# Block attention and feed-forward on one core: loads merged over the two heads of a pair, DMA transposes merged over two pairs, and the value-row transfers issued by SyncE

## The chip, the cores and the metric

The kernel runs on one core of a Trainium2 chip. The metric is the device time of one execution in microseconds (us), lower is better. Three executions of the kernel before took 244.21, 245.65 and 247.01 us, median 245.65. A further execution was recorded by the profiler: 244.68 us in all, of which its trace covers a span of 242.9 us. All times below are counted from the start of that span.

## The reference

Attention over 4 batches of 8 heads, 768 tokens and 64 channels, with a narrow local window (distance below 16) and 24 block summaries beside it; then a feed-forward block over the 3072 tokens with 512 channels in, 2048 hidden and 512 out.

```
k_sum = k.reshape(B, H, nb, 32, D).max(axis=3)          # 24 blocks of 32 keys
v_sum = v.reshape(B, H, nb, 32, D).mean(axis=3)
scores_l = scale * q @ k^T, kept where |i - j| < 16
scores_s = scale * q @ k_sum^T + log(32)
a = softmax(concat(scores_l, scores_s))
x = a @ concat(v, v_sum)
h = x @ w_in;  out = (h * sigmoid(1.702 * h)) @ w_out   # f32 in, f32 out
```

## The kernel before, in words

The work is cut into 8 half batches, u = 0 to 7 (loop at line 896): batch b = u // 2, half = u % 2, each with 384 tokens of all 8 heads. The heads are handled as 4 pairs, p = 0 to 3, since two heads of 64 channels fill 128 partitions.

For each half batch TensorE does first the **in-projection** (ff_in, line 651: tiles ph, 16 hidden tiles of 4 matmuls over the 4 pairs' rows xT) and then the **out-projection** (ff_out, line 679: tiles po, 12 pieces numbered i = 1 to 12 in the loop, four for each of 3 row blocks ms). The attention of the *next* half batch is laid between the pieces of the out-projection, by a table written by hand:

```
plan = {0: ["s0", "s1"], 3: ["v0", "s2", "s3"], 4: ["d0"], 5: ["v1", "d1"]}
```

Here s is the scores of a pair (scores, line 599: TensorE, then the exponential on ScalarE, then the mask on VectorE), v the values of two pairs (values, line 609: TensorE, then the division on VectorE into the tile x), and d the transpose of x by a DMA on SyncE's queue (dx, line 646) into xT, which the next in-projection reads. The first half batches turn x on TensorE instead ("x" in their own tables).

From the third batch on, the inputs of batch b + 1 are made ready while batch b is worked on:

- **Loads** on SyncE's queue: load_k in the out-projection of the second half of batch b - 1 after its first piece, load_v after its eighth piece, load_q only in the first half of batch b, between the transposes of the keys. Each tensor of a batch is 8 loads of 192 KB, one for each head (lines 82 to 114).
- **Casts** to bf16 on GpSimd: keys into kb, values straight into the row table vw, queries into qb.
- **Transposes** by DMA on SyncE's queue: xk (line 566) makes two for each pair, one for each half of the partitions, into kx; xq (line 573) makes one for each pair into qT, at the start of the second half. rest_k (line 577) then puts block maxima and neighbour columns into kx on VectorE.
- **Value rows**: vrows (line 336) sums the value blocks on TensorE (vsum) and VectorE (block_sums, into vs), and copies neighbour rows (vw from vw, 4 transfers) and summary rows (vw from vs, 2 transfers) by DMAs on GpSimd's queue.

Every engine works in the order of the program. SyncE does nothing but issue DMAs, in order: one that is not ready, or that takes long to issue, holds up all that stand behind it. The framework also lets each of SyncE's DMAs wait for the one issued eight places before it. All operations go through one wrapper, so the profile gives nearly all of them line L27; they are told apart by tiles.

Of the kernel before, what the change touches and what calls it, by code (L numbers as in the profile page):

```python
# [10 lines left out]
BF16 = mybir.dt.bfloat16  # L11
# [23 lines left out]
def kernel(  # L35
# [10 lines left out]
    B, H, S, D = q.shape  # L46
# [5 lines left out]
    NP = H // 2  # L52
# [17 lines left out]
    keep = ctx.enter_context(tc.tile_pool(name="keep", bufs=1))  # L70
    stage = ctx.enter_context(tc.tile_pool(name="stage", bufs=1))
    castp = ctx.enter_context(tc.tile_pool(name="cast", bufs=4))
    attp = ctx.enter_context(tc.tile_pool(name="att", bufs=4))
    outp = ctx.enter_context(tc.tile_pool(name="outp", bufs=3))
    psb = ctx.enter_context(tc.tile_pool(name="psb", bufs=2, space=bass.MemoryType.PSUM))
# [3 lines left out]

    raw = {}  # L80

    def load_k(b, p):
        t = stage.tile([128, 2, 2, JH, D], F32, name=f"kf{p}", tag=f"kf{p}")
        for i in range(2):
            if b == 0:
                sp.dma_start(out=t[:, i].rearrange("p h r d -> p h (r d)"),
                             in_=k[b, 2 * p:2 * p + 2, i * HALF:(i + 1) * HALF]
                             .rearrange("h (p r) d -> p h (r d)", r=JH))
            else:
                sp.dma_start(out=t[:, i].rearrange("p e r d -> p (e r) d"),  # L90
                             in_=k[b, 2 * p + i].rearrange("(j p) d -> p j d", p=128))
        raw["k", p] = t

    def load_q(b, p, half=None):
        if half is None:
            t = stage.tile([128, 2, NJ, D], F32, name=f"qf{p}", tag=f"qf{p}0")
            for hh in range(2):
                sp.dma_start(out=t[:, hh],
                             in_=q[b, 2 * p + hh].rearrange("(j p) d -> p j d", p=128))
            raw["q", p] = t  # L100
            return
        t = stage.tile([128, 2, JH, D], F32, name=f"qf{p}{half}", tag=f"qf{p}{half}")
        sp.dma_start(out=t.rearrange("p h r d -> p h (r d)"),
                     in_=q[b, 2 * p:2 * p + 2, half * HALF:(half + 1) * HALF]
                     .rearrange("h (p r) d -> p h (r d)", r=JH))
        raw["q", p, half] = t

    def load_v(b):
        for p in range(NP):
            t = stage.tile([128, 2, NJ, D], F32, name=f"vf{p}", tag=f"vf{p}")  # L110
            for hh in range(2):
                sp.dma_start(out=t[:, hh],
                             in_=v[b, 2 * p + hh].rearrange("(j p) d -> p j d", p=128))
            raw["v", p] = t


# [53 lines left out]
    def finish_masks():  # L170
        masks()

        for t in (0, 4, 6, 8, 10):
# [2 lines left out]
        sel(mk[32:64, NQ - 1, :], 15, 0, -1)  # L176


    kx = [[keep.tile([128, NQ, 128], BF16, name=f"kx{p}_{s}") for s in range(2)]
          for p in range(NP)]  # L180
    qT = [[keep.tile([128, S], BF16, name=f"qT{p}_{s}") for s in range(2)]
          for p in range(NP)]
    vw = [keep.tile([128, NQ, H, VC], BF16, name=f"vw{s}") for s in range(2)]
    vs = keep.tile([128, H, VC], BF16, name="vs")
    vs4 = keep.tile([128, H, VC], BF16, name="vs4")
# [48 lines left out]
                       in_=wo[:, c * 4:(c + 1) * 4, :])  # L234


    cast = {}

    def copy(eng, out, in_):
        if eng is act:  # L240
# [7 lines left out]
    def cast_k(eng, p, half=None):  # L248
        if ("k", p) in cast:
            t = cast["k", p]  # L250
        else:
            t = castp.tile([128, 2, JH, 2, D], BF16, name="kb", tag="kb")
        if half is None:
            copy(eng, t.rearrange("p e r h d -> p h (e r) d"),
                 raw["k", p].rearrange("p h e r d -> p h (e r) d"))
        else:
            copy(eng, t[:, half].rearrange("p r h d -> p h r d"), raw["k", p][:, half])
        cast["k", p] = t
# [4 lines left out]
            cast["q", p, half] = cast.pop(("q", p))  # L263

    def cast_q(eng, p, half=None):
        n = NJ if half is None else JH
        t = castp.tile([128, n, 2, D], BF16, name="qb", tag=f"qb{n}")
        copy(eng, t.rearrange("p r h d -> p h r d"),
             raw[("q", p) if half is None else ("q", p, half)])
        cast["q", p] = t  # L270
# [47 lines left out]
    def halo_dmas(w5, j0):  # L318
        halo_odd(w5, j0)
        halo_even(w5, j0)  # L320
# [15 lines left out]
    def vrows(s):  # L336
        w5 = vw[s].rearrange("p (j e) h c -> p j e h c", e=2)
        halo_odd(w5, 0, pool)
        vsum(s, range(NJ))
        block_sums()  # L340
        halo_even(w5, 0, pool)
        sum_dmas(w5, 0, pool)

    def vrows0():

# [217 lines left out]
        key_rows(p, s, ks)  # L563


    def xk(p, s):
        k4 = kx[p][s].rearrange("p (j e) c -> p j e c", e=2)
        src = cast.pop(("k", p)).rearrange("p e r h d -> p (e r h d)")
        for e in range(2):
            sp.dma_start(out=k4[:, :, e, e * 64:e * 64 + 64],  # L570
                         in_=src[e * 64:e * 64 + 64], transpose=True)

    def xq(p, s):
        sp.dma_start(out=qT[p][s].rearrange("p (j c) -> p j c", c=128),
                     in_=cast.pop(("q", p)).rearrange("p r h d -> p (r h d)"), transpose=True)

    def rest_k(p, s):
        ks = attp.tile([128, nb], BF16, name="ks", tag="ks")
# [317 lines left out]
    for u in range(2 * B):  # L896
        b, half = u // 2, u % 2
        todo = {}
        if u == 0:
            for p in range(NP):  # L900
                cast_q(dve, p, 1)
                todo[4 + p] = [lambda p=p: (q_turn(p, 1), q_copy(p, dve, 1))]
        elif u == 1:
            s = 1
            todo = {2: [lambda: tk(0, s)], 4: [lambda: tk(1, s)],
                    6: [lambda: tk(2, s)], 8: [lambda: tk(3, s)],
                    14: [lambda: halo_odd(w51, 0), lambda: vsum(s, range(NJ))],
                    15: [lambda: block_sums(), lambda: halo_even(w51, 0),
                         lambda: sum_dmas(w51, 0)]}
            for p in range(NP):  # L910
                cast_k(pool, p)
            for p in range(NP):
                cast_v(pool, s, p, 0)
                cast_v(pool, s, p, 1)
            for p in range(NP):
                cast_q1(p)
        elif half == 0 and b + 1 < B:
            s = (b + 1) % 2
            for p in range(NP):
                cast_k(pool, p)  # L920
                xk(p, s)
                if p == 1:
                    for pp in range(NP):
                        load_q(b + 1, pp)
            for p in range(NP):
                cast_v(pool, s, p, 0)
                cast_v(pool, s, p, 1)
            for p in range(NP):
                cast_q(pool, p)
        elif b + 1 < B:  # L930
            s = (b + 1) % 2
            todo = {1: [lambda: xq(0, s), lambda: xq(1, s), lambda: rest_k(0, s)],
                    2: [lambda: xq(2, s), lambda: xq(3, s), lambda: rest_k(1, s)],
                    6: [lambda: rest_k(2, s)], 8: [lambda: rest_k(3, s)]}
# [12 lines left out]
        if nxt:  # L947
            exp_soon()
        i = 0
        order = [(ms, part) for ms in range(JH) for part in range(4)]  # L950
        if u == 0:

            order = [(ms, part) for part in range(4) for ms in range(JH)]
        for ms, part in order:
            if nxt or ms < JH - 1:
                ff_out(u, ms, part)
            elif part == 0:
                ff_last(u, ms)
            if nxt:
                beside(u + 1, i)  # L960
            i += 1
            if u == 0 and i == 1:

                sp.dma_start(out=hold, in_=w_out_sb[0:16, NT - 5, 0:16])
                for p in range(NP):
                    load_k(1, p)
                load_v(1)
                for p in range(NP):
                    load_q(1, p, 0)
                    load_q(1, p, 1)  # L970
            elif half and b + 2 < B and i == 1:
                for p in range(NP):
                    load_k(b + 2, p)
            elif half and b + 2 < B and i == 8:
                load_v(b + 2)
            elif half == 0 and 0 < b < B - 1 and i == 10:
                vrows((b + 1) % 2)


# [28 lines left out]
```

## Time and profile before

| | |
|---|---|
| Median of three runs | 245.65 us (244.21 to 247.01) |
| Profiled execution | 244.68 us, span 242.9 us |
| TensorE busy | 212.7 us, 88% of the span |
| ScalarE, VectorE, GpSimd busy | 137.2, 91.2, 73.7 us |
| Chain that ended last, shares of the span | PE 70%, DMA 12%, DVE 6%, ACT 4%, SyncE's queue 4% |
| of this, the transposes into xT | 7% |
| Moved by DMA | 37.36 MB, 31.50 MB of it on the hardware queue |

The page cuts the span into 40 slices. TensorE's busy digit is 9 in nearly all of them after the first sixth, and falls to 0 and 5 in the neighbouring slices around 106 us and 5 and 0 around 167 us. The chain that ended last follows the work back from the last instruction, at each step to what released it. "SPq" is the issuing of a DMA by SyncE, and the time of a row there runs from the start of its first issue to the end of its last, waits between them included.

### The profile page before, as it was taken

Reading aid. Unit: us, or ns where it says so; the run is one execution under the profiler, and the core shown is the slowest. Engines: PE = TensorE matmul, PEld = TensorE weight load, DVE = VectorE, ACT = ScalarE, POOL = GpSimd, SP = SyncE. Lnnn points to the kernel's source line nnn. Section 1 sums busy time; section 2 is a strip of 40 time slices with the busy share of each in tenths; the row PEclk is TensorE's granted clock in tenths of the full one; section 3 lists DMA queues with packets and bytes.
Section 4 is the critical chain, followed back from the end, with each engine's and each line's share of the span. In section 5 each row is a group of like instructions: output and inputs, shape, how many; then the busy total and the mean of one; then the engine's idle time right before and its main releaser. Section 6 shows DMA issues by size and latency. Waiting matters only on the chain.

```text
span 242.9 us, 5099 instructions
## 1 busy us (share of the span) xinstructions
PE 212.7 (88%) x1989; PEld 119.0 (49%) x1989; DVE 91.2 (38%) x262; ACT 137.2 (56%) x241; POOL 73.7 (30%) x176
## 2 busy tenths in 40 slices
PE   6588899999999999905999999950999999999994
PEld 2556564556554654302555465520465455546543
DVE  5898931559756007470007001673003500530000
ACT  2697466656766788100787278610378557837610
POOL 4569970259434542710230063280000000000000
PEclk9999999999999999975899999995699999999999
DMA  6999999999999979799942795969900510141012
GB/s 172 302 230 234 206 221 178 234 206 263 286 213 219 225 155 209 123 132 238 221 71 78 182 214 110 200 101 183 208 14 0 122 75 0 46 109 45 0 43 86
DMA packets 94487, 37.36 MB, mean 154 GB/s; under 512 B 79664, under 2 KB 91184, under 8 KB 94464
## 3 DMA queue, kind: packets, MB, share of 16 engines
q1 hardware_dynamic: 89600, 31.50, 62.7%
q0 software_dynamic: 4864, 5.55, 14.0%
q8 instruction: 15, 0.25, 0.4%
q14 instruction: 8, 0.07, 0.1%
HBM read 27.26 MB, written 6.29 MB: 138 GB/s over the span
## 4 chain that ended last, share of the span: by engine, by line
PE 70%; DMA 12%; DVE 6%; ACT 4%; SPq 4%; issue 2%; POOL 0%; DVEq 0%; POOLq 0%; ACTq 0%
PE ph L27 31%; PE po L27 31%; DMA xT<-x 7%; SPq L27 4%; PE ps_av L27 3%; PE ps_s L27 2%; DMA vf<-in_v_dram 2%; DMA kf<-in_k_dram 2%; DVE kx L27 1%; DMA qf<-in_q_dram 1%; DVE a_sb L27 1%; ACT a_sb L27 1%; PE ps_k L27 1%; ACT kx L27 1%; PE ps_q L27 1%
## 5 line engine op out<-in xcount | busy, mean ns | idle before, releaser
L27 PE MATMUL ph<-xT,w_in_sb 128*128 128x384 bf16 x512 | 90.8, 337 | 19.1 <-DMA xT<-x 18.6
L27 ACT ACTIVATE gT<-ph 128x384 bf16<-128x384 f32 x128 | 61.9, 490 | 50.0 <-PE ph L27 49.3
L27 PE MATMUL po<-w_out_sb,gT 128*128 128x512 bf16 (+2 forms) x400 | 89.0, 371 | 0.0
L27 PEld LDWEIGHTS <-w_in_sb 128*128 128x128 bf16 x512 | 50.8, 101 | 55.1 <-issue 24.8
L27 PEld LDWEIGHTS <-gT 128*128 128x128 bf16 x400 | 36.4, 98 | 38.5
L27 DVE TENSOR_TENSOR a_sb<-a_sb,mk 128x768 bf16<-128x768 bf16 x32 | 18.6, 585 | 95.4 <-ACT a_sb L27 94.0
L27 ACT ACTIVATE osb<-po 128x512 f32<-128x512 f32 (+1 forms) x24 | 14.2, 592 | 37.1 <-PE po L27 37.1
L27 POOL CAST vw<-vf 128x768 bf16<-128x768 f32 (+3 forms) x35 | 24.8, 736 | 25.3 <-DMA vf<-in_v_dram 24.8
L27 ACT ACTIVATE a_sb<-ps_s 128x768 bf16<-128x768 f32 x32 | 24.3, 806 | 6.7 <-PE ps_s L27 6.7
L27 POOL CAST kb<-kf 128x768 bf16<-128x768 f32 (+1 forms) x13 | 10.6, 817 | 39.2 <-DMA kf<-in_k_dram 29.9
L27 ACT ACT_TABLE_LOAD x16 | 20.5, 1283 | 1.1 <-PEq L992 0.8
L27 POOL CAST qb<-qf 128x384 bf16<-128x384 f32 (+1 forms) x18 | 11.5, 651 | 20.6 <-DMA qf<-in_q_dram 17.4
L27 DVE TENSOR_TENSOR x<-ps_av,rc 128x384 bf16<-128x384 f32 x28 | 15.6, 558 | 1.0
L27 DVE TENSOR_REDUCE ks<-kx 128x24 bf16<-128x768 bf16 x12 | 11.3, 942 | 2.2 <-DMA kx<-kb 2.1
L27 PEld LDWEIGHTS <-a_sb 128*64 128x64 bf16 x384 | 7.9, 111 | 6.9 <-issue 3.8
L27 PE MATMUL ps_av<-vw,a_sb 128*64 128x65 bf16 x384 | 9.9, 198 | 0.4 <-DVE a_sb L27 0.4
L27 DVE COPY osb<-po 128x128 f32<-128x128 f32 x1 | 0.3, 291 | 24.9 <-PE po L27 24.9
L27 DVE COPY kx<-kx 128x80 bf16<-128x80 bf16 (+4 forms) x52 | 9.3, 230 | 0.9 <-ACT kx L27 0.9
L27 PE MATMUL ps_s<-qT,kx 64*128 64x64 bf16 x384 | 9.2, 191 | 0.5 <-ACT qT L27 0.2
L27 PEld LDWEIGHTS <-kx 64*128 64x128 bf16 x384 | 7.0, 95 | 4.8 <-issue 4.0
L27 PEld LDWEIGHTS <-warm 128*128 128x128 bf16 x71 | 5.3, 106 | 7.2 <-issue 5.6
L27 DVE RECIPROCAL rc<-ps_av 128x6 f32<-128x6 f32 x32 | 6.1, 189 | 7.2 <-PE ps_av L27 7.2
(72 smaller groups left out, 123.8 us busy)
## 6 DMA issues: line engine op xcount, KB each, us to landing
kf<-in_k_dram SPq DMA_DIRECT2D x32, 192.0 KB, 3.8
qf<-in_q_dram SPq DMA_DIRECT2D x32, 192.0 KB, 3.9
vf<-in_v_dram SPq DMA_DIRECT2D x32, 192.0 KB, 4.7
out_dram<-osb SPq DMA_DIRECT2D x23, 256.0 KB, 4.4
w_in_sb<-in_moe_w_in_dram POOLq DMA_DIRECT2D x4, 512.0 KB, 7.7
w_out_sb<-in_moe_w_out_dram POOLq DMA_DIRECT2D x4, 512.0 KB, 15.6
vw<-vs POOLq DMA_DIRECT2D x4, 148.5 KB, 7.2
vw<-vw POOLq DMA_DIRECT2D x4, 99.0 KB, 4.1
```

The lines of the kernel that those rows point to most:

```text
L27: r = f(*a, **kw)
```

## The change

- load_k and load_v (for batches 1 to 3) and load_q (for batches 2 and 3) make one load for both heads of a pair: 4 loads of 384 KB for each tensor.
- kx and qT become one tile for all four pairs for each parity of the batch, and the casts of two pairs go into one tile (kb2, qb2), so that xk and xq make one transfer for two pairs: 4 instead of 8 for the keys, 2 instead of 4 for the queries.
- load_q moves ahead: it follows load_v directly, in the half batch before.
- xq moves ahead: from the start of the second half to the tenth piece of the out-projection of the first half.
- The six value-row transfers of batches 2 and 3 are issued by SyncE, behind xq, instead of GpSimd.
- rest_k of the second pair stands one place later (after hidden tile 3 instead of 2).

The core of the diff:

```diff
     def load_k(b, p):
         t = stage.tile([128, 2, 2, JH, D], F32, name=f"kf{p}", tag=f"kf{p}")
-        for i in range(2):
-            if b == 0:
+        if b:
+            sp.dma_start(out=t.rearrange("p h e r d -> p (h e r) d"), in_=chunks(k, b, p))
+        else:
...
     def load_q(b, p, half=None):
         if half is None:
             t = stage.tile([128, 2, NJ, D], F32, name=f"qf{p}", tag=f"qf{p}0")
-            for hh in range(2):
-                sp.dma_start(out=t[:, hh],
-                             in_=q[b, 2 * p + hh].rearrange("(j p) d -> p j d", p=128))
+            sp.dma_start(out=t.rearrange("p h j d -> p (h j) d"), in_=chunks(q, b, p))
...
-    def xk(p, s):
-        k4 = kx[p][s].rearrange("p (j e) c -> p j e c", e=2)
-        src = cast.pop(("k", p)).rearrange("p e r h d -> p (e r h d)")
+
+    def xk(g, s):
+        k4 = kxs[s].rearrange("p i (j e) c -> p (i j) e c", e=2)
+        src = kb2[g].rearrange("p i e r h d -> p (i e r h d)")
         for e in range(2):
-            sp.dma_start(out=k4[:, :, e, e * 64:e * 64 + 64],
+            sp.dma_start(out=k4[:, 2 * g * NJ:2 * (g + 1) * NJ, e, e * 64:e * 64 + 64],
                          in_=src[e * 64:e * 64 + 64], transpose=True)
...
             for p in range(NP):
                 cast_k(pool, p)
-                xk(p, s)
-                if p == 1:
-                    for pp in range(NP):
-                        load_q(b + 1, pp)
+                if p % 2:
+                    xk(p // 2, s)
...
-            todo = {1: [lambda: xq(0, s), lambda: xq(1, s), lambda: rest_k(0, s)],
-                    2: [lambda: xq(2, s), lambda: xq(3, s), lambda: rest_k(1, s)],
+            todo = {1: [lambda: rest_k(0, s)], 3: [lambda: rest_k(1, s)],
                     6: [lambda: rest_k(2, s)], 8: [lambda: rest_k(3, s)]}
...
             elif half and b + 2 < B and i == 8:
                 load_v(b + 2)
+                for p in range(NP):
+                    load_q(b + 2, p)
             elif half == 0 and 0 < b < B - 1 and i == 10:
-                vrows((b + 1) % 2)
+                s = (b + 1) % 2
+                vsum(s, range(NJ))
+                block_sums()
+                xq(0, s)
+                xq(1, s)
+                w5 = vw[s].rearrange("p (j e) h c -> p j e h c", e=2)
+                halo_dmas(w5, 0)
+                sum_dmas(w5, 0)
```

SyncE has 166 rows in its order before and 134 with the change. Two places of that order carry the prediction.

The first is SyncE's queue in the half batch u = 2, ahead of the two transposes into xT that the in-projection of u = 3 reads (kf, vf, qf are loaded inputs, kb and qb their casts, osb a store's source; the numbers at the ends of names are buffers). Before, from the loads of the third pair's queries on:

```order
L27 DMA qf_1555<-in_q_dram 128x6x64 [waits DMAHW4_49]
L27 DMA qf_1555<-in_q_dram 128x6x64 [waits DMAHW5_49]
L27 DMA qf_1558<-in_q_dram 128x6x64 [waits DMAHW6_49]
L27 DMA qf_1558<-in_q_dram 128x6x64 [waits DMAHW7_49]
L27 DMA_TRANSPOSE kx_0_98<-kb 128x6x64 [waits DMAHW0_49,Pool_49]
L27 DMA_TRANSPOSE kx_0_98<-kb 128x6x64 [waits DMAHW1_49]
L27 DMA_TRANSPOSE kx_0_100<-kb 128x6x64 [waits DMAHW2_49,Pool_49]
L27 DMA_TRANSPOSE kx_0_100<-kb 128x6x64 [waits DMAHW3_49]
L27 DMA out_dram<-osb 128x512 [waits DMAHW4_49,Activation_49]
L27 DMA_TRANSPOSE xT_119<-x_1760 128x6x128 [waits DMAHW5_49,DVE_49,PE_49]
L27 DMA_TRANSPOSE xT_120<-x_1836 128x6x128 [waits DMAHW6_49,DVE_49,PE_49]
```

and with the change, from the second pair's queries on:

```order
L27 DMA qf_1453<-in_q_dram 128x12x64 [waits DMAHW4_49,Pool_49]
L27 DMA qf_1455<-in_q_dram 128x12x64 [waits DMAHW5_49,Pool_49]
L27 DMA qf_1457<-in_q_dram 128x12x64 [waits DMAHW6_49,Pool_49]
L27 DMA out_dram<-osb 128x512 [waits DMAHW7_49,Activation_49]
L27 DMA_TRANSPOSE kx_97<-kb 128x12x64 [waits DMAHW0_49,Pool_49]
L27 DMA_TRANSPOSE kx_97<-kb 128x12x64 [waits DMAHW1_49]
L27 DMA_TRANSPOSE kx_97<-kb 128x12x64 [waits DMAHW2_49,Pool_49]
L27 DMA_TRANSPOSE kx_97<-kb 128x12x64 [waits DMAHW3_49]
L27 DMA out_dram<-osb 128x512 [waits DMAHW4_49,Activation_49]
L27 DMA_TRANSPOSE xT_110<-x_1719 128x6x128 [waits DMAHW5_49,DVE_49,PE_49]
L27 DMA_TRANSPOSE xT_111<-x_1795 128x6x128 [waits DMAHW6_49,DVE_49,PE_49]
```

The query loads no longer stand between the key transposes: they stand ahead of all of these, right behind the value loads, one for each pair and twice as large. The key transposes are half as many and of 12 column blocks instead of 6; the transposes into xT are the same and keep their place behind them.

The second place is the end of the same out-projection. Before, GpSimd's order, from the last two query casts on:

```order
L27 CAST qb<-qf_1555 128x2x6x64 [waits DMAHW5_49,DMAHW4_49]
L27 CAST qb<-qf_1558 128x2x6x64 [waits DMAHW7_49,DMAHW6_49]
L27 DMA vw_110<-vw_110 16x6x528 [waits DMASW0_49,Pool_49]
L27 DMA vw_110<-vw_110 16x5x528 [waits DMASW1_49]
L27 DMA vw_110<-vw_110 16x5x528 [waits DMASW2_49,PE_49]
L27 DMA vw_110<-vw_110 16x6x528 [waits DMASW3_49]
L27 DMA vw_110<-vs 24x6x528 [waits DMASW4_49,DVE_49]
L27 DMA vw_110<-vs 24x6x528 [waits DMASW5_49]
L27 CAST kb<-kf_2072 128x2x6x64 [waits DMAHW6_49,DMAHW5_49]
```

and with the change SyncE's order, from the store behind the transposes into xT on:

```order
L27 DMA out_dram<-osb 128x512 [waits DMAHW7_49,Activation_49]
L27 DMA_TRANSPOSE qT_99<-qb 128x12x128 [waits DMAHW0_49,Pool_49]
L27 DMA_TRANSPOSE qT_99<-qb 128x12x128 [waits DMAHW1_49,Pool_49]
L27 DMA vw_101<-vw_101 16x6x528 [waits DMAHW2_49]
L27 DMA vw_101<-vw_101 16x5x528 [waits DMAHW3_49]
L27 DMA vw_101<-vw_101 16x5x528 [waits DMAHW4_49,PE_49]
L27 DMA vw_101<-vw_101 16x6x528 [waits DMAHW5_49]
L27 DMA vw_101<-vs 24x6x528 [waits DMAHW6_49,DVE_49]
L27 DMA vw_101<-vs 24x6x528 [waits DMAHW7_49]
L27 DMA out_dram<-osb 128x512 [waits DMAHW0_49,Activation_49]
L27 DMA kf_2029<-in_k_dram 128x12x64 [waits DMAHW1_49]
L27 DMA kf_2031<-in_k_dram 128x12x64 [waits DMAHW2_49]
```

The six value-row transfers left GpSimd for SyncE, where they now stand behind the two query transposes, which wait for GpSimd's query casts, and ahead of a store and of the next key loads. In GpSimd's order the next key casts follow the query casts directly.

## Rows read from the trace of the kernel before

**Rows 1.** Chain that ended last, in order of time: start us, us, what.

```profile
102.72 9.49 DMA xT<-x
...
129.12 0.50 PE ps_av L27 x24
...
137.77 10.40 PE ph L27 x64
...
162.60 7.53 DMA xT<-x
```

**Rows 2.** Timeline, PE: start us, us, engine, operation, count, [idle before <-releaser].

```profile
112.34 12.76 PE L27 MATMUL ph<-xT,w_in_sb 128*128 128x384 bf16 x64 [9.39 <-DMA xT<-x]
...
170.27 12.81 PE L27 MATMUL ph<-xT,w_in_sb 128*128 128x384 bf16 x64 [8.88 <-DMA xT<-x]
```

**Rows 3.** Stretches: length; busy (count) by engine; PEclk, DMA share, GB/s.

```profile
106.60:112.30 5.70, 0.00 (x0) 0.00 (x0) 1.07 (x5) 0.00 (x0) 0.00 (x0) 0.50 1.10 118
112.30:116.80 4.50, 4.46 (x15) 2.06 (x16) 0.00 (x0) 1.40 (x3) 0.00 (x0) 0.50 1.08 275
116.80:125.10 8.30, 8.30 (x52) 5.01 (x51) 0.00 (x0) 5.95 (x13) 3.21 (x4) 1.00 1.04 185
```

**Rows 4.** Timeline, SyncE's queue, u = 2 and its borders.

```profile
76.73 5.96 SPq L27 DMA_DIRECT2D vf<-in_v_dram  x8
82.79 0.79 SPq L27 DMA_DIRECT2D out_dram<-osb  x1
83.68 5.13 SPq L27 DMA_TRANSPOSE kx<-kb  x4
88.86 6.44 SPq L27 DMA_DIRECT2D qf<-in_q_dram  x8
95.40 6.51 SPq L27 DMA_TRANSPOSE kx<-kb  x4
102.01 0.60 SPq L27 DMA_DIRECT2D out_dram<-osb  x1
102.72 5.73 SPq L27 DMA_TRANSPOSE xT<-x  x2
```

**Rows 5.** Timeline, SyncE's queue, in u = 3 and in u = 4.

```profile
131.02 4.00 SPq L27 DMA_TRANSPOSE xT<-x  x2
...
135.70 6.00 SPq L27 DMA_DIRECT2D vf<-in_v_dram  x8
```

**Rows 6.** SyncE's issues by tile: ns min/median/max; us to landing.

```profile
L27 SPq DMA_TRANSPOSE xT<-x x11: 1211/1224/3937, 73.9 to 214.9; - x11
...
DMA to landing us min/median/max: 2.8/3.7/7.5
...
L27 SPq DMA_TRANSPOSE kx<-kb x16: 1204/1253/3176, 83.7 to 160.6; - x16
```

**Rows 7.** Timeline, GpSimd, the casts of u = 2.

```profile
81.06 1.60 POOL L27 CAST vw<-vf 128x768 bf16<-128x768 f32 x2 [4.08 <-DMA vf<-in_v_dram]
...
86.47 1.60 POOL L27 CAST vw<-vf 128x768 bf16<-128x768 f32 x2 [0.26 <-DMA vf<-in_v_dram]
93.46 0.83 POOL L27 CAST qb<-qf 128x768 bf16<-128x768 f32 x1 [5.39 <-DMA qf<-in_q_dram]
...
98.85 0.83 POOL L27 CAST qb<-qf 128x768 bf16<-128x768 f32 x1 [0.78 <-DMA qf<-in_q_dram]
```

**Rows 8.** Timeline, VectorE: the last x of u = 3.

```profile
97.51 0.56 DVE L27 TENSOR_TENSOR x<-ps_av,rc 128x384 bf16<-128x384 f32 x1
```

**Rows 9.** Value rows: GpSimd's issues in u = 2, SyncE's in u = 1.

```profile
99.62 1.09 POOL L27 DMA_DIRECT2D vw<-vw  x2
...
60.83 3.67 SPq L27 DMA_DIRECT2D vw<-vw  x4
64.61 1.70 SPq L27 DMA_DIRECT2D vw<-vs  x2
```

**Rows 10.** SyncE's issues by tile, vw: us to landing.

```profile
DMA to landing us min/median/max: 3.9/5.3/5.5
```

More of the change, by code (lines that the diff above doesn't have):

```diff
@@ L72 @@
     castp = ctx.enter_context(tc.tile_pool(name="cast", bufs=4))
+    castp2 = ctx.enter_context(tc.tile_pool(name="cast2", bufs=2))
     attp = ctx.enter_context(tc.tile_pool(name="att", bufs=4))
@@ L80, with chunks @@
     raw = {}
+    def chunks(x, b, p):
+        return x[b, 2 * p:2 * p + 2].rearrange("h s d -> (h s) d").rearrange("(a p) d -> p a d", p=128)
     def load_k(b, p):
         t = stage.tile([128, 2, 2, JH, D], F32, name=f"kf{p}", tag=f"kf{p}")
-        for i in range(2):
-            if b == 0:
+        if b:
+            sp.dma_start(out=t.rearrange("p h e r d -> p (h e r) d"), in_=chunks(k, b, p))
+        else:
+            for i in range(2):
                 sp.dma_start(out=t[:, i].rearrange("p h r d -> p h (r d)"),
@@ L88, in load_k @@
                              .rearrange("h (p r) d -> p h (r d)", r=JH))
-            else:
-                sp.dma_start(out=t[:, i].rearrange("p e r d -> p (e r) d"),
-                             in_=k[b, 2 * p + i].rearrange("(j p) d -> p j d", p=128))
         raw["k", p] = t
@@ L110, in load_v @@
             t = stage.tile([128, 2, NJ, D], F32, name=f"vf{p}", tag=f"vf{p}")
-            for hh in range(2):
-                sp.dma_start(out=t[:, hh],
-                             in_=v[b, 2 * p + hh].rearrange("(j p) d -> p j d", p=128))
+            if b:
+                sp.dma_start(out=t.rearrange("p h j d -> p (h j) d"), in_=chunks(v, b, p))
+            else:
+                for hh in range(2):
+                    sp.dma_start(out=t[:, hh],
+                                 in_=v[b, 2 * p + hh].rearrange("(j p) d -> p j d", p=128))
             raw["v", p] = t
@@ L176, in finish_masks @@
         sel(mk[32:64, NQ - 1, :], 15, 0, -1)
[L179 to L182, printed above, removed]
+    kxs = [keep.tile([128, NP, NQ, 128], BF16, name=f"kx{s}") for s in range(2)]
+    kx = [[kxs[s][:, p] for s in range(2)] for p in range(NP)]
+    qTs = [keep.tile([128, NP, S], BF16, name=f"qT{s}") for s in range(2)]
+    qT = [[qTs[s][:, p] for s in range(2)] for p in range(NP)]
     vw = [keep.tile([128, NQ, H, VC], BF16, name=f"vw{s}") for s in range(2)]
@@ L234, in load_w_out @@
                        in_=wo[:, c * 4:(c + 1) * 4, :])
-    cast = {}
+    cast, kb2, qb2 = {}, {}, {}
     def copy(eng, out, in_):
@@ L251, in cast_k @@
         else:
-            t = castp.tile([128, 2, JH, 2, D], BF16, name="kb", tag="kb")
+            if p % 2 == 0:
+                kb2[p // 2] = castp2.tile([128, 2, 2, JH, 2, D], BF16, name="kb", tag="kb")
+            t = kb2[p // 2][:, p % 2]
         if half is None:
@@ L265, in cast_q @@
     def cast_q(eng, p, half=None):
-        n = NJ if half is None else JH
-        t = castp.tile([128, n, 2, D], BF16, name="qb", tag=f"qb{n}")
+        if half is None:
+            if p % 2 == 0:
+                qb2[p // 2] = castp2.tile([128, 2, NJ, 2, D], BF16, name="qb", tag="qb")
+            t = qb2[p // 2][:, p % 2]
+        else:
+            t = castp.tile([128, JH, 2, D], BF16, name="qb", tag="qb")
         copy(eng, t.rearrange("p r h d -> p h r d"),
@@ L334, in sum_dmas @@
         eng.dma_start(out=w5[0:nb, j0:NJ, 1], in_=rows)
[L336 to L342, printed above, removed]
     def vrows0():
@@ L563, in tk, with xq @@
         key_rows(p, s, ks)
-    def xk(p, s):
-        k4 = kx[p][s].rearrange("p (j e) c -> p j e c", e=2)
-        src = cast.pop(("k", p)).rearrange("p e r h d -> p (e r h d)")
+    def xk(g, s):
+        k4 = kxs[s].rearrange("p i (j e) c -> p (i j) e c", e=2)
+        src = kb2[g].rearrange("p i e r h d -> p (i e r h d)")
         for e in range(2):
-            sp.dma_start(out=k4[:, :, e, e * 64:e * 64 + 64],
+            sp.dma_start(out=k4[:, 2 * g * NJ:2 * (g + 1) * NJ, e, e * 64:e * 64 + 64],
                          in_=src[e * 64:e * 64 + 64], transpose=True)
-    def xq(p, s):
-        sp.dma_start(out=qT[p][s].rearrange("p (j c) -> p j c", c=128),
-                     in_=cast.pop(("q", p)).rearrange("p r h d -> p (r h d)"), transpose=True)
+    def xq(g, s):
+        sp.dma_start(out=qTs[s][:, 2 * g:2 * g + 2].rearrange("p i (j c) -> p (i j) c", c=128),
+                     in_=qb2[g].rearrange("p i j h d -> p (i j h d)"), transpose=True)
     def rest_k(p, s):
```

## The prediction

> **What bounds the kernel now.** I read the chain of waits first, then TensorE's timeline around the places the chain named, then the granted clock there, and last the queue that held the named transfer back. The chain runs through TensorE's matmuls nearly all the way after the first 26 us, except at two places where it goes through a transpose into xT: 9.49 us from 102.72 and 7.53 us from 162.60 [rows 1]. TensorE's timeline shows the same as idle time: the in-projections of u = 3 and u = 5 start only at 112.34 and 170.27, after 9.39 and 8.88 us of standing still for xT [rows 2]. Each stall costs more than its idle time. [...] So the two places cost 9.39 + 8.88 = 18.27 us of idleness and 2.36 + 2.41 = 4.77 us of slow clock, 23.04 us in all. Elsewhere TensorE is busy without a gap worth naming, so this is the most that a change on the queues can give.
>
> Why is xT late? The second x of u = 3 is ready at 97.51 + 0.56 = 98.07 [rows 8], but its transpose is issued only behind everything that SyncE has in front of it. From 76.73 to 108.45 SyncE issues without a pause: 8 value loads, a store, 4 key transposes, 8 query loads, 4 key transposes, a store, and then the two transposes into xT [rows 4]. In u = 3, where no loads or key transposes stand ahead, the same two transposes begin at 131.02 [rows 5] and the following in-projection starts on time at 137.77 [rows 1]. So it is the place in SyncE's queue that makes the stall, not the transposes themselves.
>
> **The change, part by part, at the first stall.**
>
> *Loads.* The bytes stay the same, the queries now follow the values directly. Values land at a steady pace: the casts of the first and fourth pair start at 81.06 and 86.47, which is 1.80 us for each pair; the queries keep the same pace, 93.46 to 98.85 [rows 7]. I let four more pairs follow at that pace: the last queries are there at 86.47 + 4 x 1.80 = 93.7, 5.2 us earlier than now. SyncE's last value load was issued by 76.73 + 5.96 = 82.69 [rows 4], 3.8 us before the cast that waited for it; with the same lead it has issued the last query load at 89.9. That leaves 13.2 us for 8 merged issues. A single load takes 0.75 us of the queue now (5.96 / 8), a merged one at most twice that, 8 x 1.5 = 12 us, so the price of one issue is covered by the pace of the transfers either way; without that cover it would be paid in full. The store behind them ends at 90.7.
>
> *Key transposes.* This is the unknown. A merged transpose has twice the column blocks, and no such shape is in the trace. Now they take 5.13 us for four in the first batch, 1.28 us each, and 6.51 us for the four that come right behind loads, 1.4 us more [rows 4]. The lower end for a merged one is today's 1.25 us, if the price is for the instruction; the upper end is twice that, 2.5 us. The key transposes read 64 partitions and the ones into xT 128, yet their shortest issues are 1204 and 1211 ns [rows 6]. What the two share is six column blocks, and a merged one has twelve; so I take 2.0 us, nearer to the upper end. Four of them plus the 1.4 us behind loads is 9.4 us: done at 100.1, the store at 100.7.
>
> *Transposes into xT.* They are unchanged: 1.2 us of issue and 2.8 to 3.7 us from issue to landing [rows 6]. The first, issued at 100.7, lands at 103.5 to 104.4; the second, at 101.9, lands at 104.7 to 105.6. TensorE is done with u = 2 at 112.34 - 9.39 = 102.95 and has 1.0 us of matmuls (6 of 64 in 10.40 us) before it needs the second. It waits 0.6 to 1.5 us, plus 0.2; I take 1.3 us. With 1.25 us for a key transpose there is no wait at all; with 2.5 us it is up to 3.7 us.
>
> *Value rows.* SyncE now issues them, behind xT: after the second xT (103.1), a store (103.7) and two query transposes at 2.0 us each (107.7). GpSimd's casts that these need end at 94.5, so they do not block. Then, at the prices of the same six transfers on SyncE in u = 1, 3.67 + 1.70 us [rows 9]: issued by 113.1, the last one landed 5.5 us [rows 10] after its start, at 117.8. The values that read them start at 129.12 now [rows 1], and 9.39 + 2.36 us earlier if the stall goes, plus the 1.3 us left: 118.7. That covers it with 0.9 us to spare; with the longest landing of any transpose, 7.5 us [rows 6], they would be 1.1 us late. I take nothing. On GpSimd these transfers start at 99.62 [rows 9], so they share the DMA engines with xT; one transpose into xT took 3937 ns to issue where the usual is 1224 [rows 6]. Behind xT in the same queue they cannot do that, and that is why I use the undisturbed landing. [...] If xT kept its longest landing of 7.5 us, it would cost about 5.4 us at the first place and 5.9 at the second, the clock loss would stay, and the time would be 238 us.
>
> *The rest* costs nothing: rest_k one place later is VectorE work that nothing waits for soon, and the merged tiles leave TensorE's, VectorE's and ScalarE's orders as they were.
>
> **The second stall** repeats this. The loads begin at 135.70 [rows 5], u = 4 ends at 170.27 - 8.88 = 161.39: 25.7 us, against 102.95 - 76.73 = 26.2 us at the first. So the wait is 0.5 us longer, 1.8 us.
>
> **The sum.** 23.04 us of loss, less 1.3 + 1.8 us that stay, is 19.9 us. The profiled execution took 244.68 us, so 224.8 us; the median of the runs shown, 245.65, is 1.0 us above it. I say 225.0. With the low end for the transposes it is 221.6, with the high one 244.68 - 23.04 + 3.7 + 4.2 = 229.5.
>
> **The rivals.**
>
> *The merged transposes issue at twice the time, and the wait lowers the clock.* For it: the equal times at six blocks; and waits of 9 us did lower the clock. Against it: nothing shows that a wait of 4 us does. Time: 229.5, with the clock loss 234.3. Chance 0.20. [...]
>
> *The DMA engines are the bound, not the queue.* Then the same bytes ahead of xT bring it as late as now: 245. For it: a DMA share around 1 in the stall [rows 3]. Against it: GpSimd's casts stood 5.39 us without queries [rows 7] while SyncE was issuing transposes, so the transfers had room. Chance 0.07.
>
> *Slower.* A merged transpose issues much worse than twice. Now the second xT is issued by 102.72 + 5.73 = 108.45. With a price T it is issued by 90.7 + 1.4 + 4T + 0.6 + 2.4 = 95.1 + 4T, which is later than now from T = 3.3 us on. At 3.94 us, the longest issue that any row shows, it would be 2.4 us later at each place: 249.5. Chance 0.06.
>
> *Something else in SyncE's order holds part back*, most likely the value rows or query transposes of u = 4: 235 to 243. Chance 0.07.
>
> My forecast, 221 to 229, has 0.60. A range of 221 to 234 takes in the first rival. A measurement of this kernel can tell about 1%, 2.5 us, from no change. Faster by more than that: 0.60 + 0.20 + 0.07 = 0.87; within: 0.07; slower: 0.06.
>
> **What would show it.** TensorE's waits for xT ahead of u = 3 and u = 5 under 2 us each; both in-projections near 10.4 us and no stretch at 0.50 there; query casts that follow the value casts without the 5.39 us; key transposes near 2.0 us each; no new wait of TensorE's values for vw. A key transpose at 2.5 us or more, waits of 4 us or a low clock behind them would make the prediction wrong on the slow side, and xT landing near 112 wrong altogether.

## The result and the profile after

| | before | changed |
|---|---|---|
| Median (range, runs) | 245.42 us (244.21 to 247.01, 4) | 224.12 us (222.85 to 225.67, 4) |
| Ratio, 95% interval | | 0.9132 [0.9051, 0.9212] |
| Profiled execution, span | 244.68, 242.9 us | 222.85, 221.2 us |
| TensorE's mean granted clock | 0.958 | 0.998 |

The change takes 8.7% off the time. Some runs fell in a slower state, and every ratio compares fast runs only, so a ratio can differ a little from the quotient of two medians. The page of the changed kernel (busy time by engine, 40 slices of the span, shares of the chain that ended last) has no hole in TensorE's row after the first slices and no slice below 9 in the granted clock:

```profile
PE 209.1 (95%) x1989; PEld 118.2 (53%) x1989; DVE 92.0 (42%) x262; ACT 136.7 (62%) x241; POOL 66.4 (30%) x164
...
PE   7488999999999999999999999999999999999993
...
PEclk9999999999999999999999999999999999999999
...
PE 77%; DVE 9%; DMA 6%; ACT 4%; issue 2%; SPq 1%; DVEq 0%; ACTq 0%
```

TensorE's timeline (start, us, operation, count, idle before) shows the place of [rows 2]. Of the 9.39 us of waiting 0.23 us are left ahead of the in-projection of u = 3, and the values that read the moved value rows start without any wait:

```profile
103.06 10.56 PE L27 MATMUL ph<-xT,w_in_sb 128*128 128x384 bf16 x64 [0.23 <-DMA xT<-x]
...
117.56 0.57 PE L27 MATMUL ps_av<-vw,a_sb 128*64 128x65 bf16 x24
...
150.66 10.56 PE L27 MATMUL ph<-xT,w_in_sb 128*128 128x384 bf16 x64
```

The last row is the in-projection of u = 5. It has no bracket, so nothing was waited for, where 8.88 us were lost before. Both blocks take 10.56 us instead of 12.76 and 12.81. The stretches of these two blocks (columns as in [rows 3]) run at full clock, with a DMA share (last but one) of 0.99 and 0.89, not much below the 1.10 of the old stall:

```profile
103.00:113.60 10.60, 10.54 (x65) 6.38 (x66) 4.39 (x20) 7.60 (x16) 0.00 (x0) 1.00 0.99 177
150.80:161.20 10.40, 10.40 (x66) 6.26 (x64) 4.60 (x20) 7.73 (x16) 0.00 (x0) 1.00 0.89 180
```

SyncE's queue in u = 2, which answers to [rows 4], tells why:

```profile
76.56 5.32 SPq L27 DMA_DIRECT2D vf<-in_v_dram  x4
81.98 7.06 SPq L27 DMA_DIRECT2D qf<-in_q_dram  x4
89.14 1.70 SPq L27 DMA_DIRECT2D out_dram<-osb  x1
90.92 6.78 SPq L27 DMA_TRANSPOSE kx<-kb  x4
97.80 0.69 SPq L27 DMA_DIRECT2D out_dram<-osb  x1
98.60 3.79 SPq L27 DMA_TRANSPOSE xT<-x  x2
102.48 0.53 SPq L27 DMA_DIRECT2D out_dram<-osb  x1
103.10 3.41 SPq L27 DMA_TRANSPOSE qT<-qb  x2
106.56 3.10 SPq L27 DMA_DIRECT2D vw<-vw  x4
109.77 1.70 SPq L27 DMA_DIRECT2D vw<-vs  x2
```

The eight merged loads take 12.4 us (5.32 + 7.06), as the sixteen single ones did (5.96 + 6.44 in [rows 4]), but the key transposes 6.78 us instead of 5.13 + 6.51. The first xT is issued 4.1 us earlier, at 98.60 against 102.72, while the in-projection starts 9.3 us earlier. The other half lies in the transfers: the chain that ended last has 4.33 us from the issue of this xT to its landing, and had 9.49 us in [rows 1]. The chain's row, then SyncE's issues by tile (columns as in [rows 6]):

```profile
98.60 4.33 DMA xT<-x
```

```profile
L27 SPq DMA_TRANSPOSE xT<-x x11: 1211/1228/2457, 73.9 to 193.0; - x11
...
L27 SPq DMA_TRANSPOSE kx<-kb x8: 1262/1462/2406, 90.9 to 143.8; - x8
...
L27 SPq DMA_TRANSPOSE qT<-qb x4: 1466/1637/1838, 103.1 to 151.6; - x4
```

So two candidates stand beside each other: fewer transposes in front of xT, and no transfers of GpSimd beside it. The first eight experiments separate them, the last three put them together again.

### The profile page after: what moved, and what is told of

It is laid out like the page before. It is cut to its first block, busy times and chain, and to the rows that moved or that the text cites. A ratio compares the mean times of both kernels' runs of the same rounds, so it can differ in the third digit from the quotient of the medians.

```text
span 221.2 us, 5025 instructions
## 1 busy us (share of the span) xinstructions
PE 209.1 (95%) x1989; PEld 118.2 (53%) x1989; DVE 92.0 (42%) x262; ACT 136.7 (62%) x241; POOL 66.4 (30%) x164
## 2 busy tenths in 40 slices
DMA packets 94407, 37.36 MB, mean 169 GB/s; under 512 B 78704, under 2 KB 91440, under 8 KB 94384
## 4 chain that ended last, share of the span: by engine, by line
PE 77%; DVE 9%; DMA 6%; ACT 4%; issue 2%; SPq 1%; DVEq 0%; ACTq 0%
PE ph L27 37%; PE po L27 30%; DMA xT<-x 4%; PE ps_av L27 3%; DVE a_sb L27 3%; PE ps_s L27 2%; DMA kf<-in_k_dram 2%; DVE kx L27 2%; ACT a_sb L27 1%; DVE qT L27 1%; PE ps_k L27 1%; ACT kx L27 1%; PE ps_q L27 1%; PE ps_vt L27 1%; PE ps_x L27 1%
## 5 line engine op out<-in xcount | busy, mean ns | idle before, releaser
L27 PE MATMUL ph<-xT,w_in_sb 128*128 128x384 bf16 x512 | 86.3, 326 | 1.2 <-DMA xT<-x 0.7
L27 PEld LDWEIGHTS <-w_in_sb 128*128 128x128 bf16 x512 | 49.4, 98 | 34.0 <-issue 1.5
L27 DVE TENSOR_TENSOR a_sb<-a_sb,mk 128x768 bf16<-128x768 bf16 x32 | 19.5, 622 | 75.5 <-ACT a_sb L27 74.2
L27 POOL CAST vw<-vf 128x768 bf16<-128x768 f32 (+3 forms) x35 | 24.3, 718 | 15.9 <-DMA vf<-in_v_dram 15.5
```

The lines of the kernel that those rows point to most:

```text
L27: r = f(*a, **kw)
```

## Experiments

My theory was that the number of transposes and the place of the value rows share the gain, and that merged and earlier loads give nothing. The rivals were that the loads' count or place counts, and that one of the two causes is the whole gain. Ratios are to the kernel before, run on the same chip (its medians there: 245.39 us for the first four, 245.46 for the next four, 244.21 for the last three). The first four undo one part of the change each.

**The loads single again.** load_k, load_q and load_v make one load for each head; all else as changed.

```diff
-            sp.dma_start(out=t.rearrange("p h j d -> p (h j) d"), in_=chunks(q, b, p))
+            for hh in range(2):
+                sp.dma_start(out=t[:, hh],
+                             in_=q[b, 2 * p + hh].rearrange("(j p) d -> p j d", p=128))
...
```

> The changed kernel with two loads for each pair again (16 issues in a row instead of 8 ahead of the key transposes). Theory: SyncE issues loads at the pace at which the DMA engines take them, so the number of issues is covered; 16 x 0.75 = 12 us against the 12.5 us that the 8 merged ones took. Time within 1 us of the changed kernel, TensorE's waits for xT under 0.5 us. Rival, that merged loads are what freed the queue: 8 more issues at 0.55 us put the key transposes 4.4 us later, waits of 3 to 4 us at each of the two places, 230 to 232 us, or 235 if the clock falls behind them.

Measured: 223.47 us (222.26 to 225.75), 0.9098 [0.9025, 0.9172], not to be told from the changed kernel. SyncE's timeline shows the cover:

```profile
77.08 6.08 SPq L27 DMA_DIRECT2D vf<-in_v_dram  x8
83.27 7.13 SPq L27 DMA_DIRECT2D qf<-in_q_dram  x8
```

The in-projections of u = 3 and u = 5 start without a wait. Sixteen single loads take 13.2 us of the queue, eight merged ones 12.4. A merged load is issued in about twice the time (12.4 / 8 = 1.55 us against 13.2 / 16 = 0.83), so merging frees almost nothing. That the loads run at the pace of the transfers and not of the issues is my estimate from these two sums.

**The transposes single again.** One transfer for each pair.

```diff
-        src = kb2[g].rearrange("p i e r h d -> p (i e r h d)")
-        for e in range(2):
+        for i in range(2):
+            src = kb2[g][:, i].rearrange("p e r h d -> p (e r h d)")
+            for e in range(2):
...
-        sp.dma_start(out=qTs[s][:, 2 * g:2 * g + 2].rearrange("p i (j c) -> p (i j) c", c=128),
+        for i in range(2):
+            sp.dma_start(out=qTs[s][:, 2 * g + i].rearrange("p (j c) -> p j c", c=128),
```

> The changed kernel with one DMA transpose for each pair again (8 key transposes instead of 4, 4 query transposes instead of 2). Theory: the price is for the instruction, about 1.3 us of SyncE's queue, whatever its size; 4 more key transposes put the first xT 5.2 us later, at 103.8, landing at 106.6 to 107.5: waits of 3.5 to 4.5 us at both places, 230 to 232 us, and 235 to 236 if the granted clock falls behind such a wait too. Rival, that the time came from the rows' move or the queries' place: under 1 us of change, since both stay.

Measured: 234.79 us (233.81 to 235.65), 0.9588 [0.9514, 0.9663], 10.7 us slower than the changed kernel. SyncE's timeline:

```profile
92.42 11.44 SPq L27 DMA_TRANSPOSE kx<-kb  x8
...
104.58 2.58 SPq L27 DMA_TRANSPOSE xT<-x  x2
```

Eight key transposes hold the queue 11.44 us, four merged ones 6.78. TensorE's timeline shows what that costs:

```profile
80.21 12.25 PE L27 MATMUL ph<-xT,w_in_sb 128*128 128x384 bf16 x64 [2.20 <-DMA xT<-x]
...
107.45 1.14 PE L27 MATMUL ph<-xT,w_in_sb 128*128 128x384 bf16 x6 [1.42 <-DMA xT<-x]
...
160.65 11.83 PE L27 MATMUL ph<-xT,w_in_sb 128*128 128x384 bf16 x64 [5.05 <-DMA xT<-x]
```

The wait of 2.20 us stands ahead of any merged transpose, at a place where the changed kernel waits 0.52 us, and 1.2 us in a second profiled execution of it. So up to 3.4 us of this run (1.7 of wait, 1.7 of slower matmuls) cannot be put down to the queue as the edit changes it. The wait there differs from run to run; its cause is open.

**The value rows back on GpSimd.**

```diff
+                halo_odd(w5, 0, pool)
...
-                halo_dmas(w5, 0)
-                sum_dmas(w5, 0)
+                halo_even(w5, 0, pool)
+                sum_dmas(w5, 0, pool)
```

> The changed kernel with the value-row transfers on GpSimd's queue again. They can start once GpSimd's last query cast is done, at about 95.6, and run beside the transposes into xT (98.6 to 102.4). If SyncE's queue alone made the stall: within 1 us of the changed kernel. If the rows' large packets hold xT up in the DMA engines: each xT takes 2 to 4 us longer to issue or land, waits of 2 to 5 us at both places, 227 to 233 us, up to 237 with a low clock.

Measured: 232.06 us (231.15 to 233.93), 0.9475 [0.9404, 0.9546], 7.9 us slower than the changed kernel, although SyncE has six DMAs fewer to issue. SyncE's timeline at the first place:

```profile
99.72 2.82 SPq L27 DMA_TRANSPOSE xT<-x  x2
...
103.25 12.16 SPq L27 DMA_TRANSPOSE qT<-qb  x2
```

Two query transposes take 12.16 us, and 3.41 us in the changed kernel. GpSimd issues the last four value-row transfers just ahead of them (GpSimd's timeline):

```profile
101.83 1.06 POOL L27 DMA_DIRECT2D vw<-vw  x2 [4.74 <-PE ps_vs L27]
103.05 1.24 POOL L27 DMA_DIRECT2D vw<-vs  x2 [0.15 <-issue]
```

TensorE's waits for xT at this first place stay small, 0.49 and 0.52 us, so the rows did not hold xT up by 2 to 4 us in both places as expected. At the second place GpSimd's rows (from 151.36) coincide with xT itself (issued from 150.75), and TensorE stands still for it (TensorE's timeline):

```profile
154.90 1.78 PE L27 MATMUL ph<-xT,w_in_sb 128*128 128x384 bf16 x6 [2.03 <-DVE kx L27]
158.44 11.36 PE L27 MATMUL ph<-xT,w_in_sb 128*128 128x384 bf16 x58 [1.77 <-DMA xT<-x]
```

Both blocks run in part at the lower clock (0.50 from 155.30 to 162.00). The first row names kx as the releaser, but by tile the two xT of this place take 4.0 and 6.3 us to land, so the first is there at 154.8: TensorE waited for xT. In the changed kernel the in-projection of u = 5 starts 3.95 us after the issue of its first xT (150.66 and 146.71) and has no wait. In this run the value rows' transfers slowed the transposes beside them: 12.16 us for two query transposes, 3.41 in the changed kernel, and 6.3 us for the landing of an xT.

**The query loads at their old place**, still merged.

```diff
                 if p % 2:
                     xk(p // 2, s)
+                if p == 1:
+                    for pp in range(NP):
+                        load_q(b + 1, pp)
...
-                for p in range(NP):
-                    load_q(b + 2, p)
```

> The changed kernel with the (merged) query loads at their old place, between the key transposes of the first and the second two pairs. Theory: the queue holds the same instructions ahead of xT, in another order, and the first two key transposes are issued while the value loads still land; the last key transpose ends within 2 us of where it does in the changed kernel (97.8): within 1.5 us of its time. Rival, that the earlier query loads made the gain: waits of 4 to 5 us at both places, 231 to 236 us.

Measured: 223.28 us (222.59 to 224.24), 0.911 [0.9051, 0.9169]: the place of the query loads is worth nothing that can be measured, in a kernel with the rows on SyncE.

The next four go on from there: each of the two causes alone, neither, and the rows on a third queue. On their chip the kernel before scatters more, from 242.69 to 248.40 us, so the sizes are less sure.

**The kernel before with the value rows on SyncE**, and nothing else; the first two of the six transfers stand behind the value sums now, as in the change.

```diff
-        halo_odd(w5, 0, pool)
         vsum(s, range(NJ))
         block_sums()
-        halo_even(w5, 0, pool)
-        sum_dmas(w5, 0, pool)
+        halo_odd(w5, 0)
+        halo_even(w5, 0)
+        sum_dmas(w5, 0)
```

> The kernel before with one edit: the value-row transfers on SyncE's queue, behind the transposes into xT. SyncE's queue ahead of xT stays as long as it was, so the first xT is still issued at about 102.7; without the rows beside it each takes 1.25 us and lands 2.8 to 3.7 us later, the second at about 107 instead of 112. Theory of two causes: waits of 3.5 to 4.5 us remain at both places, 230 to 236 us depending on the clock behind them. If the queue's length alone were the cause: 243 us or more. If the rows alone were: 226 us or less.

Measured: 230.15 us (229.84 to 231.64), 0.9441 [0.9357, 0.9525]. SyncE's and then TensorE's timeline:

```profile
103.03 2.59 SPq L27 DMA_TRANSPOSE xT<-x  x2
```

```profile
105.90 1.14 PE L27 MATMUL ph<-xT,w_in_sb 128*128 128x384 bf16 x6 [1.86 <-DVE kx L27]
...
156.70 11.93 PE L27 MATMUL ph<-xT,w_in_sb 128*128 128x384 bf16 x64 [3.14 <-DVE kx L27]
```

This is the clearest single result. The two xT are issued from 103.03, no earlier than in the kernel before (102.72 in [rows 4]), 0.8 us earlier if both are counted from the start of the value loads (77.81 and 76.73), yet the in-projection starts at 105.90 instead of 112.34. Only the transfers got faster: two issues in 2.59 us instead of 5.73. The rows name kx as the releaser, but 103.03 plus the 2.79 us that this kernel's chain has for the landing of the second xT is 105.82: TensorE waited for xT here too, and the name is that of the last event the profile could see. With 1.86 and 3.14 us the waits are shorter than the 3.5 to 4.5 us expected.

**The kernel before with merged transposes**, and nothing else; the tiles and casts that the merging needs, and the bodies of xk and xq, are those of the change.

```diff
-                xk(p, s)
+                if p % 2:
+                    xk(p // 2, s)
...
```

> The kernel before with merged transposes alone (loads single, query loads and query transposes at their old places, value rows on GpSimd's queue). Theory of two causes: the key transposes leave SyncE about 5 us earlier, the first xT is issued at about 98 and only its end meets GpSimd's rows (from 99.6): waits of 1 to 5 us at both places, 227 to 234 us. If the merging alone made the gain: 226 us or less. If it needs the rows' move to be worth anything: 240 us or more.

Measured: 227.53 us (224.35 to 229.33), 0.9221 [0.9078, 0.9365]. Merged transposes bring xT's issue forward, to the moment at which GpSimd starts the value rows, 97.18 (SyncE's and TensorE's timeline):

```profile
97.29 3.61 SPq L27 DMA_TRANSPOSE xT<-x  x2
```

```profile
104.07 1.14 PE L27 MATMUL ph<-xT,w_in_sb 128*128 128x384 bf16 x6 [2.31 <-DMA xT<-x]
```

xT is issued 1.3 us earlier than in the changed kernel and still arrives 1 us later. At the second place the rows start 0.7 us behind xT (149.67 and 149.00), and TensorE did not wait. The four runs scatter from 224.35 to 229.33 us, which fits a meeting that falls differently from run to run; that is an argument, not a measurement.

**Neither**: the changed kernel with single transposes and with the value rows on GpSimd, so that merged loads, earlier query loads and earlier query transposes are left. The edit is the two shown above, of the transposes and of the rows, together.

> The changed kernel with both undone, single transposes and value rows on GpSimd's queue; loads stay merged, query loads and query transposes early. If the two effects add, 224.1 + 10.7 + 7.9 = 242.7 us; theory: 239 to 246 us. If they overlap (either alone already pays what both would): 235 us or less.

Measured: 241.0 us (240.72 to 241.73), 0.9882 [0.9786, 0.9978]. Most of the old stall is back (TensorE's timeline):

```profile
110.39 11.99 PE L27 MATMUL ph<-xT,w_in_sb 128*128 128x384 bf16 x64 [7.38 <-DMA xT<-x]
...
166.04 13.16 PE L27 MATMUL ph<-xT,w_in_sb 128*128 128x384 bf16 x64 [7.25 <-DMA xT<-x]
```

From the changed kernel the two causes nearly add: 10.7 and 7.9 us apart, 16.9 us together. From the kernel before they overlap: by the ratios the rows alone take 5.6% off and the merged transposes alone 7.8%, the whole change 8.7%, since a wait that is gone cannot be shortened again. The parts left in this kernel are worth 1.2% (0.2 to 2.1%) beside the kernel before; which of them is open.

**The value rows on ScalarE's queue**, the rest as changed.

```diff
-                halo_dmas(w5, 0)
-                sum_dmas(w5, 0)
+                halo_odd(w5, 0, act)
+                halo_even(w5, 0, act)
+                sum_dmas(w5, 0, act)
```

> The changed kernel with the value rows on ScalarE's queue instead of SyncE's, so that they run beside the query transposes, and cost ScalarE about 4 us of issue in each of the two half batches. If any second queue beside a DMA transpose slows it: merged query transposes of 4 us or more on SyncE (6.2 and 5.9 beside GpSimd's rows, 1.5 and 1.8 with the rows behind them), 228 to 233 us. If it is the packets that GpSimd's transfers are cut into (4224 bytes at 0.4 to 0.6 us each): query transposes under 2.5 us, and a time within 3 us of the changed kernel, the rest being ScalarE's issue.

Measured: 229.55 us (229.03 to 229.78), 0.9401 [0.9332, 0.947]. This was to tell whether it is GpSimd's kind of transfer or any transfer beside a transpose that hurts. The four query transposes took 1.9 to 3.1 us to issue, between the changed kernel's 1.5 to 1.8 and the 2.2 to 6.2 with the rows on GpSimd. But xT itself is late beside ScalarE's rows, so it is not GpSimd's kind of transfer alone. At the second place (SyncE's, ScalarE's, then TensorE's timeline) the first matmuls start 4.5 us after the first xT's issue, and a second wait for xT follows, where the changed kernel has none:

```profile
150.22 2.91 SPq L27 DMA_TRANSPOSE xT<-x  x2
```

```profile
150.36 4.87 ACTq L27 DMA_DIRECT2D vw<-vw  x4
```

```profile
154.75 1.14 PE L27 MATMUL ph<-xT,w_in_sb 128*128 128x384 bf16 x6 [0.50 <-DMA xT<-x]
156.93 1.14 PE L27 MATMUL ph<-xT,w_in_sb 128*128 128x384 bf16 x6 [1.04 <-DMA xT<-x]
```

How much worse GpSimd's transfers are than ScalarE's stays open. The rest of what the run costs comes from elsewhere: ScalarE's next output tile starts only when its last DMA is issued, 9.03 us after its last one at the first place, and TensorE waits for it, 1.83 us at the first place and 1.30 us at the second (ScalarE's, then TensorE's timeline at the first place):

```profile
98.34 6.30 ACTq L27 DMA_DIRECT2D vw<-vw  x4
105.62 2.24 ACTq L27 DMA_DIRECT2D vw<-vs  x2
107.90 0.60 ACT L27 ACTIVATE osb<-po 128x512 f32<-128x512 f32 x1 [9.03 <-DMA vw<-vs]
```

```profile
108.55 8.61 PE L27 MATMUL ph<-xT,w_in_sb 128*128 128x384 bf16 x52 [1.83 <-ACT osb L27]
```

The last three kernels belong together.

**The two edits alone**: the kernel before with merged transposes and with the rows on SyncE; loads single, query loads and query transposes at their old places.

> The kernel before with two edits alone: merged transposes, and the value rows on SyncE's queue; loads single, query loads and query transposes at their old places. Theory: these two are the whole gain; waits for xT under 1 us at both places, within 1.5 us of the changed kernel run beside it (about 224). If merged or earlier loads, or the earlier query transposes, carry a part: 227 us or more.

Measured: 223.71 us (223.28 to 224.78), 0.9186 [0.9143, 0.9228]. TensorE waits for neither xT (its timeline):

```profile
103.38 10.56 PE L27 MATMUL ph<-xT,w_in_sb 128*128 128x384 bf16 x64
...
151.32 10.56 PE L27 MATMUL ph<-xT,w_in_sb 128*128 128x384 bf16 x64
```

**The change once more**, beside it.

> The changed kernel once more, as the measure for the two runs beside it: 222.5 to 226 us.

Measured: 223.51 us (222.33 to 224.86), 0.9168 [0.9124, 0.9211]. The intervals overlap: these two edits are the whole gain that can be measured.

How the gain divides between the two depends on what else stands in the kernel. On top of merged transposes alone (0.9221 [0.9078, 0.9365]) the ratios do not tell the rows' move from nothing, and the medians give it 3.8 us; in the changed kernel it is worth 7.9 us. Merged transposes with the rows on GpSimd took 227.53 us (0.9221) with single loads and the queries at their old places, and 232.06 us (0.9475 [0.9404, 0.9546]) with merged loads and the queries ahead. So something among these parts, harmless with the rows on SyncE, costs time with the rows on GpSimd; which of them is not shown.

**Transposes of all four pairs in one transfer**, 24 column blocks.

```diff
-            sp.dma_start(out=k4[:, 2 * g * NJ:2 * (g + 1) * NJ, e, e * 64:e * 64 + 64],
+            sp.dma_start(out=k4[:, :, e, e * 64:e * 64 + 64],
...
```

> The changed kernel with the transposes of all four pairs in one (2 key transposes of 24 column blocks for a batch, 1 query transpose). Theory, a price for the instruction: an undisturbed one still issues in 1.2 to 1.6 us, SyncE's queue ahead of xT is 2.6 us shorter, and since the waits there are gone already the time stays within 1.5 us of the changed kernel. If the price grows with the blocks beyond some size: issues of 2.5 us or more where nothing stands ahead, and no room won. A new wait could come from the last pair's cast, for which the single transpose waits.

Measured: 223.62 us (222.38 to 224.75), 0.9172 [0.9128, 0.9215]: not to be told from the change, since nothing is left to wait for. Its issue times (by tile, columns as in [rows 6]) are what it was for:

```profile
L27 SPq DMA_TRANSPOSE kx<-kb x4: 1597/2462/3968, 91.1 to 141.4; - x4
...
L27 SPq DMA_TRANSPOSE qT<-qb x2: 3862/4100/4339, 102.6 to 148.9; - x2
```

| Column blocks in one transpose | 6 | 12 | 24 |
|---|---|---|---|
| 64 partitions (kx), shortest issue | 1.20 us | 1.26 us | 1.60 us |
| 128 partitions (qT), shortest issue | 1.21 us | 1.47 us | 3.86 us |

Going from 6 to 12 blocks adds 0.06 and 0.26 us to the shortest issue. From 12 to 24 the two shapes part: two key transposes of 24 hold the queue 5.62 us at the first place, four of 12 took 6.78, but the one query transpose of 24 takes longer (4.34 us) than two of 12 (3.41). There are only four key and two query transposes of 24, and they stand behind other transfers in the queue, so how much is the price of the instruction and how much a wait behind the others is not shown.

## Why the prediction was right, and where it was off

Forecast 225.0 us (221 to 234), measured 224.12. The mechanism stood: both stalls and their slow clock are gone, and what held xT back was the queue ahead of it and the transfers beside it: 10.7 and 7.9 us where one of the two was undone. Step by step, with the profiled execution:

- **Loads.** Said: the last query cast at 93.7, the last load issued by 89.9, the store done at 90.7. Read: 94.71, 89.04 and 90.84. The value that the steady 1.80 us of [rows 7] gave was good to 1.0 us, and with it the reason: single loads cost the same (223.47 us with them). GpSimd's timeline has the first query cast behind 0.19 us of waiting, instead of the 5.39 us of [rows 7], and the last behind 1.90 us:

```profile
88.40 0.83 POOL L27 CAST qb<-qf 128x768 bf16<-128x768 f32 x1 [0.19 <-DMA qf<-in_q_dram]
...
94.71 0.83 POOL L27 CAST qb<-qf 128x768 bf16<-128x768 f32 x1 [1.90 <-DMA qf<-in_q_dram]
```

- **Key transposes**, the term that was mis-sized. Said: 2.0 us each, between 1.25 and 2.5, nearer to twice the price because the equal times at six blocks could mean a price for each block. Measured: 1.26 us at the shortest, against 1.20 for six blocks, so up to twelve blocks the price is nearly one for the instruction, and the four take 6.78 us where 9.4 were said. They end at 97.70 instead of 100.1. The 1.4 us behind loads were about right (6.78 less 4 x 1.26 is 1.7).
- **Transposes into xT.** Said: issued at 100.7, waits of 1.3 and 1.8 us. Read: issued at 98.60, waits of 0.23 us and none. The landing was mis-sized too, the other way: 2.8 to 3.7 us were said, and the first xT took 4.33 us, 2.46 us of it to issue. Issued at 100.7 with this landing it would have come at 105.0, and the wait would have been 2.1 us at least instead of 1.3. The cheaper key transposes hid this; it is luck that the two errors went against each other.
- **Value rows.** Said: issued by 113.1, no wait behind them. Read: issued by 111.47, values at 117.56 without a wait.
- **The sum.** 19.9 us were forecast off the profiled execution, 21.8 came. With 1.26 us for a key transpose the same working gives the low end, 221.6; the profiled execution took 222.85. Of TensorE's rows the two places give back 18.04 us of waiting and 4.45 us of slow matmuls, 22.5 us; the 0.7 us between that and 21.8 lies in small waits that I did not follow. The forecast counted 4.77 us of slow matmuls (12.76 and 12.81 us less 10.40 each, with a granted clock of 0.50 to 116.80 at the first place [rows 3] and to 174.8 at the second), 0.3 us too many: the 10.40 us of an undisturbed block in [rows 1] begin only where the work before it in the chain ends, and the timeline has 10.56 us for the same block.

The price of a block was the doubt behind the first rival, at 0.20. The issue time hardly grew from 6 to 12 blocks (1.20 to 1.26 and 1.21 to 1.47 us at the shortest), and did from 12 to 24 on 128 partitions (1.47 to 3.86 us).

The price that the prediction named for an xT that keeps its longest landing, 238 us, did not come. The kernel before with the rows on SyncE spends 4.4 us more of SyncE's time on issues at the first place (2.64 and 1.72 us, from 106.33) and is 5.6% faster: its two xT are issued in 2.59 us instead of 5.73. So here the choice of the queue also set what ran beside what. That transposes were slowed by transfers of another queue is measured; by what means is not shown.

What the prediction understated is the second cause. I named GpSimd's rows as the reason to use an undisturbed landing, and gave them no term of their own. By themselves they are worth 5.6%, where the merged transposes by themselves are worth 7.8%. The comparison with u = 3 hid them: it was to show that xT's place in the queue makes the stall, but u = 3 has neither key transposes ahead of xT nor value rows beside it. (It does have eight key loads ahead of xT; these were issued by 120.90, ten us before.) And the 238 us went by a longest landing of 7.5 us, where [rows 1] has 9.49; with that they would have been 240. The rival that the DMA engines are the bound had a part in the truth: 5.2 of the 9.3 us that the first place gained lay between the issue of xT and its landing. But the number of bytes did not set it, for both pages have 37.36 MB; what ran beside xT did.

## What to carry to other kernels

When a transfer on the critical path is late, ask two questions of it: what stands ahead of it in its own queue, and what moves beside it on the others. A longer queue that keeps side work behind the urgent transfer can beat a shorter one that lets it run beside: here 230.15 us against 245.46, by the rows' move alone. Merge DMA transposes while an issue costs nearly the same whatever its size (1.20 and 1.26 us for 6 and 12 blocks on 64 partitions), and measure where that ends (1.47 and 3.86 us for 12 and 24 on 128); merging the plain loads was not worth the code (0.9098 of the time before with single loads, 0.9132 with merged ones).

## What the runs showed of the hardware that was not expected

A wait of TensorE much shorter than the 9 us of the kernel before was followed by the lower clock too. In the kernel with single transposes these stretches lie at the waits of 2.20 and 5.05 us (columns as in [rows 3]):

```profile
81.35:84.77 3.42, 3.42 (x13) 1.67 (x11) 0.00 (x0) 1.48 (x4) 1.94 (x3) 0.50 1.39 218
...
159.90:163.20 3.30, 2.55 (x9) 1.20 (x10) 0.28 (x3) 0.00 (x0) 0.00 (x0) 0.50 0.86 197
```

Both have a granted clock of 0.50, and the blocks of 64 matmuls took 12.25 and 11.83 us. In the same run the wait of 1.42 us was not followed by one (1.00 from 100 to 110 us). Against the 10.56 us of an undisturbed block, 1.3 to 1.7 us come on top of a wait of a few us; I had priced this only for waits near 9 us, with 2.36 and 2.41 us, and as a mere chance for one of 4 us.
